# Two weight matrices cast to bf16 in flight by GpSimd's software DMA, in a linear-attention and MLP kernel on one core

## The chip, the cores and the metric

One NeuronCore of a Trainium2 chip. The time is that of the device for one execution, in microseconds (us), as the median of several executions. The profile's "span" is the stretch between the first and the last recorded instruction; it is 1.6 to 2.1 us shorter than the time. The record marks every run told here as fast: none is more than 1.5% above the quickest of its kernel.

## The reference, cut to what matters

```python
kv  = einsum('bhsd,bhse->bhde', k, v)            # batch 8, heads 8, s 576, d 64
out = einsum('bhsd,bhde->bhse', q, kv)
x   = out / rms(out) * g_norm                    # -> [8, 576, 512]
tok = einsum('ts,bsd->btd', w_tok, alpha1 * x + beta1)       # w_tok 576 x 576
u   = x + lam * tok
ch  = relu((alpha2 * u + beta2) @ w_ch1) @ w_ch2             # 512 x 2048, 2048 x 512
return u + lam * ch                              # float32
```

## The kernel before

All engines' work is put down as operations with their reads and writes, and a scheduler lays them out per engine. For the first batch (b=0) everything must be prepared: k, v and q loaded in halves, w_tok loaded and turned by matmuls with an identity, w_ch1 ("w1") and w_ch2 ("w2") loaded and cast. From the first matmul with w1 (called ch1 here) on, TensorE has real work without a break: ch1, the kv product of the second batch (b=1), the product with w2 (ch2), and so on.

```python
order = ["k0", "v0", "q0", "k1", "t0", "v1", "q1", "t1",      # SyncE's queue:
         "w0", "g", "w1", "w2", "Bk", "Bv", "t2", "w3", "Bq", "lam", "a2", "w4",
         "w5", "w6", "w7"]     # t: w_tok; w0-w3: w1's quarters; w4-w7: w2's; B: batch 1
...
def load_w(i):
    if i < 4:
        P.op("SP", 0.6, lambda e: e.dma_start(stg[:, i % 3], moe_w_ch1[...]), ...)
        for dj in range(4):                                   # casts on ACT, POOL or DVE
            P.op({"ACT": ..., "POOL": 0.66, "DVE": ...}, 0, lambda e, dj=dj: copy(
                e, w1[:, dj, 512 * i:512 * i + 512], stg[:, i % 3, dj]), ...)
        bias_groups(i)                                        # 16 matmuls, beta2 @ w1
    else:
        P.op("SP", 0.6, lambda e: e.dma_start(stg[:, i % 3], moe_w_ch2[...]), ...)
        for hh in range(4):                                   # w2 scaled by lam, on DVE or POOL
            P.op(dve_pool(512), 0, ...)
...
# kv product of one batch: 144 matmuls of 64x64, each with its weight load
m = e.matmul(t.ap(...), kf[rows, x, c], vf[rows, x, c], start=(c == 0), stop=(c == 8), ...)
...
# filler, put where TensorE would idle before ch1; a list of zeros
def warm(e, t):
    return e.matmul(t.flat()[:, 0:256], wz[:, 0:128], wz[:], start=True, stop=True)
```

## Time and profile before

| | before |
|---|---|
| time, median of 3 | 363.64 us (363.46 to 364.29) |
| span, granted clock | 362.2 us, 0.995 |
| first ch1 matmul | 33.89 us |
| kv product of b=1 starts | 43.13 us |
| first ch2 matmul | 58.31 us |
| end | 362.2 us |

The middle rows are milestones on TensorE. From 34 us on nothing on TensorE is filler, so a milestone that moves should move the end with it. The prediction below shows the busy totals, the stages and the chain.

```profile
q1 hardware_dynamic: 67472, 58.66, 59.7%
q8 instruction: 27, 0.44, 0.5%
```

### The profile page before, as it was taken

The page shows a single profiled execution, that of the slowest core. Times are in us where ns is not written, and L with a number is a line of the kernel's source. Part 1 is how long each engine was busy: PE and PEld are TensorE (multiplying, and loading weights), DVE is VectorE, ACT ScalarE, POOL GpSimd, SP SyncE. Part 2 cuts the span into 40 slices and gives each one's busy share as a digit, 9 for nine tenths or more (in the row PEclk, how much of TensorE's full clock was granted, in tenths as well). Part 3 has the DMA queues.
Part 4 walks back from the last instruction along what each step waited for, and adds up shares of the span by engine and source line. Part 5 has one row for each costly group of instructions (what it writes and reads, how often), then busy time and mean ns, then how long its engine had stood idle before and what let it go on. Part 6 is the DMA issues. An engine that isn't in the chain of part 4 may idle for free.

```text
span 362.2 us, 7967 instructions
## 1 busy us (share of the span) xinstructions
PE 353.6 (98%) x3543; PEld 213.6 (59%) x3335; DVE 207.1 (57%) x321; ACT 147.5 (41%) x262; POOL 113.1 (31%) x93
## 2 busy tenths in 40 slices
PE   7999999999999999999999999999999999999995
PEld 5888774467754554457744554457744554457644
DVE  3555799962876288723974289714883288620021
ACT  2576267037750168007830167007720156007500
POOL 4377078410252006700381016800751006300000
PEclk9899999999999999999999999999999999999999
DMA  7999996067947694667926692686746510341023
GB/s 282 364 375 338 376 365 223 0 73 128 315 156 119 107 313 162 88 128 117 381 47 134 111 352 88 116 119 194 288 66 128 115 29 2 72 93 24 2 58 87
DMA packets 67558, 59.17 MB, mean 163 GB/s; under 512 B 45552, under 2 KB 45828, under 8 KB 67524
## 3 DMA queue, kind: packets, MB, share of 16 engines
q1 hardware_dynamic: 67472, 58.66, 59.7%
q8 instruction: 27, 0.44, 0.5%
q14 instruction: 7, 0.06, 0.0%
q10 hardware_dynamic: 52, 0.01, 0.0%
HBM read 38.60 MB, written 9.44 MB: 133 GB/s over the span
## 4 chain that ended last, share of the span: by engine, by line
PE 93%; DMA 3%; DVE 1%; SPq 1%; issue 1%
PE ps L986 34%; PE ps L936 19%; PE ps L921 14%; PE ps L785 8%; PE ps L602 5%; DMA vf<-in_v_dram 3%; PE ps L397 2%; PE ps L682 2%; PE ps L1144 2%; PE ps L798 1%; PE ps L819 1%; PE ps L570 1%; PE ps L952 1%; DVE w L1268 1%; SPq L506 1%
## 5 line engine op out<-in xcount | busy, mean ns | idle before, releaser
L986 PE MATMUL ps<-w,ht 128*128 128x512 bf16 (+1 forms) x569 | 125.8, 373 | 1.8 <-issue 1.0
L986 PEld LDWEIGHTS ps<-w,ht 128*128 128x128 bf16 x592 | 56.8, 98 | 64.0 <-issue 1.2
L910 ACT ACTIVATE ht<-ps,bias 128x640 bf16<-128x640 f32 (+2 forms) x100 | 74.1, 744 | 45.8 <-PE ps L936 37.9
L936 PE MATMUL ps<-a2t,w 128*128 128x320 bf16 x512 | 71.5, 299 | 0.0
L760 POOL TENSOR_TENSOR xm<-xm,g_bc 128x1024 f32<-128x1024 f32 (+1 forms) x17 | 35.0, 2061 | 111.4 <-DVE rt L757 109.3
L936 PEld LDWEIGHTS ps<-a2t,w 128*128 128x128 bf16 x512 | 49.4, 98 | 20.2
L997 DVE TENSOR_TENSOR xm<-ps,xm 128x512 f32<-128x512 f32 (+1 forms) x33 | 22.2, 673 | 56.5 <-PE ps L986 56.4
L921 PE MATMUL ps<-a2t,w 128*128 128x512 bf16 x231 | 53.3, 380 | 0.9 <-DVE small L737 0.5
L633 ACT ACTIVATE kvd<-ps 64x256 bf16<-64x256 f32 x24 | 9.1, 378 | 101.2 <-PE ps L602 101.0
L731 DVE TENSOR_REDUCE small<-sq 128x16 f32<-128x1024 f32 (+3 forms) x30 | 25.1, 849 | 24.9 <-ACT sq L729 24.7
L921 PEld LDWEIGHTS ps<-a2t,w 128*128 128x128 bf16 x240 | 22.6, 98 | 25.7 <-DVE xm L753 0.7
L785 PE MATMUL ps<-rt,wt 128*128 128x512 bf16 x140 | 31.4, 379 | 0.0
L911 DVE TENSOR_SCALAR ht<-ps,bias 128x512 bf16<-128x512 f32 (+2 forms) x32 | 22.9, 725 | 11.4 <-PE ps L921 5.1
L729 ACT ACTIVATE sq<-ps 128x1024 f32<-128x1024 f32 (+3 forms) x30 | 21.6, 735 | 10.2 <-PE ps L397 8.2
L769 DVE TENSOR_TENSOR xm<-ps,xm 128x512 f32<-128x512 f32 x28 | 19.1, 686 | 8.0 <-PE ps L785 7.9
L785 PEld LDWEIGHTS ps<-rt,wt 128*128 128x128 bf16 x140 | 13.7, 98 | 16.5
L771 POOL TENSOR_TENSOR a2b<-xm,a_bc 128x512 bf16<-128x512 f32 x11 | 17.7, 1610 | 17.6 <-DVE xm L769 17.6
L534 POOL TENSOR_TENSOR qs<-qf,qs 128x512 bf16<-128x512 f32 x12 | 15.2, 1266 | 25.5 <-ACT qs L493 24.5
L997 DVE TENSOR_TENSOR xtl<-ps,xtl 128x512 f32<-128x512 f32 x4 | 2.8, 691 | 35.5 <-PE ps L986 35.5
L753 DVE TENSOR_TENSOR xm<-ps,small 128x1024 f32<-128x1024 f32 (+1 forms) x20 | 20.0, 1004 | 0.2
L602 PEld LDWEIGHTS ps<-vf,kf 64*64 64x64 f32 x1152 | 18.0, 137 | 3.5 <-issue 2.5
L602 PE MATMUL ps<-vf,kf 64*64 64x64 f32 x1152 | 19.3, 223 | 0.3 <-DMA vf<-in_v_dram 0.2
(105 smaller groups left out, 337.1 us busy)
## 6 DMA issues: line engine op xcount, KB each, us to landing
stg<-in_moe_w_ch_dram SPq DMA_DIRECT2D x8, 1024.0 KB, 10.9
kf<-in_k_dram SPq DMA_DIRECT2D x7, 1152.0 KB, 6.2
vf<-in_v_dram SPq DMA_DIRECT2D x7, 1152.0 KB, 9.2
qf<-in_q_dram SPq DMA_DIRECT2D x7, 1152.0 KB, 9.8
out_dram<-xm SPq DMA_DIRECT2D x62, 128.0 KB, 2.4
kf<-in_k_dram SPq DMA_DIRECT2D x2, 576.0 KB, 5.8
vf<-in_v_dram SPq DMA_DIRECT2D x2, 576.0 KB, 7.1
qf<-in_q_dram SPq DMA_DIRECT2D x2, 576.0 KB, 8.5
```

Source lines behind the costliest of these rows:

```text
L602: m = e.matmul(t.ap(slice(64 * i, 64 * i + 64))[:, y, 64 * x_:64 * x_ + 64], kf[rows, x, c], vf[rows, x, c], start=(c == 0), stop=(c == 8) ...
L729: P.op("ACT", act_us(64 * m), lambda e: e.activation(both(sqv), raw(), ACT.Square), r=[t], w=[("sq", sqs)])
L731: P.op("DVE", dve_us(64 * m), lambda e: e.tensor_reduce(out=smv, in_=sqv, axis=AX.X, op=ALU.add), r=[("sq", sqs)], w=[("sm", sms)], pri=-20)
L753: P.op("DVE", dve_us(64 * m), lambda e: e.tensor_tensor(out=x3, in0=raw(), in1=inv(), op=ALU.mult), r=[t, ("sm", sms)], w=xk, pri=-200)
L760: P.op(dve_pool(64 * m) if b < 2 else "POOL", pool_us(64 * m), lambda e: e.tensor_tensor(out=x3, in0=x3, in1=gb, op=ALU.mult), r=xk + ["g" ...
L785: m = e.matmul(t.flat(), wt[:, sc if sc < 4 else 4 + b % 2, 128 * c:128 * c + 128], rt[:, rs(b, sc), :], start=(sc == 0), stop=(sc == 4))
L910: return e.activation(dst, src(), ACT.Relu, bias=bi)
L911: return e.tensor_scalar(out=dst, in0=src(), scalar1=bi, scalar2=0.0, op0=ALU.add, op1=ALU.max)
L921: m = e.matmul(t.flat(), w1[:, dj, 128 * fj:128 * fj + 128], a2t[:, dj, 0:512], start=(dj == 0), stop=(dj == 3))
L936: m = e.matmul(t.ap()[:, i, 0:320], w1[:, dj, 128 * fj:128 * fj + 128], a2t[:, dj, 320 * i:320 * i + 320], start=(dj == 0), stop=(dj == 3))
L986: m = e.matmul(t.flat()[:, 0:m_], ht[:, fj, 128 * c:128 * c + 128], w2[:, fj, lo:hi], start=(fj == 0), stop=(fj == 15))
L997: P.op("DVE", dve_us(m_), lambda e: e.tensor_tensor(out=x, in0=t.flat()[:, 0:m_], in1=x, op=ALU.add), r=[t] + keys, w=keys)
```

## The change

Intent: w_tok and w1 leave SyncE's queue. GpSimd loads them with software DMAs that cast float32 to bf16 on the way, so the 16 casts of w1 vanish and w_tok can be turned by bf16 matmuls, one pass where float32 takes two. So that these loads get bandwidth, SyncE's loads of the second batch, and all that follow in its queue, are held until w1's second quarter is in.

```diff
@@ load of k, v, q
+                after=P.lastw[("w1", 1)] if b == 1 else [],
@@ SyncE's order
-        order = ["k0", "v0", "q0", "k1", "t0", "v1", "q1", "t1",
-                 "w0", "g", "w1", "w2", "Bk", "Bv", "t2", "w3", "Bq", "lam", "a2", "w4",
-                 "w5", "w6", "w7"]
+        order = ["k0", "v0", "q0", "k1", "v1", "q1",
+                 "g", "Bk", "Bv", "lam", "a2", "w4",
+                 "Bq", "w5", "w6", "w7"]
@@ w_tok (and its last part, wst4, likewise)
-                P.op("SP", 0.6, lambda e, u=u: e.dma_start(
+                P.op("POOL", 0.5, lambda e, u=u: e.dma_start(
                     wst[:, u, :], wrows[u % 2, :, u // 2:u // 2 + 7:2]),
@@ turning w_tok
-                                ident[0:rr, 0:rr], start=True, stop=True,
+                                identb[0:rr, 0:rr], start=True, stop=True,
@@ load_w, w1's quarters
-                P.op("SP", 0.6, lambda e: e.dma_start(stg[:, i % 3], moe_w_ch1[...
-                for dj in range(4):
-                    P.op({"ACT": ..., "POOL": 0.66, "DVE": ...}, 0, ... copy(...
+                P.op("POOL", 0.9, lambda e: e.dma_start(
+                    w1[:, :, 512 * i:512 * i + 512], moe_w_ch1[
+                        :, 512 * i:512 * i + 512].rearrange("(j p) f -> p j f", p=128)),
+                    w=[("w1", i)], dma_us=2.6, at=-9000.0 + i, after=P.lastw[gate[i]])
```

Cut: the bf16 tiles, the gates of the new loads, and the scheduler's model of a second DMA queue. Lines move by about 14: L602 is L616 after, L952 L966, L986 L1000, L1144 L1159, L1165 L1180, L1213 L1228, L1334 L1345.

## The prediction

> **What bounds the kernel now.** I read the page's first two parts first: one busy total per engine, then the forty slices.
>
> ```profile
> PE 353.6 (98%) x3543; PEld 213.6 (59%) x3335; DVE 207.1 (57%) x321; ACT 147.5 (41%) x262; POOL 113.1 (31%) x93
> PE   7999999999999999999999999999999999999995
> PEclk9899999999999999999999999999999999999999
> DMA  7999996067947694667926692686746510341023
> ```
>
> TensorE is busy throughout, so the end moves only if TensorE has less to do or starts its necessary work earlier. But some of "busy" is filler: the program multiplies zeros (L1334) to keep the clock up until the first ch1 matmul (L952). So next I read busy time by stage (the loads' first wait, the preparation up to ch1, the rest), and then the filler alone for the same stages:
>
> ```profile
> 0.00:13.50 13.50, 11.35 (x142) 9.14 (x142) 4.80 (x13) 5.33 (x12) 3.88 (x16) 1.00 0.88 320
> 13.50:34.00 20.50, 20.44 (x272) 17.99 (x273) 12.50 (x35) 13.72 (x32) 15.72 (x17) 0.92 0.98 347
> 34.00:362.00 328.00, 321.85 (x3133) 186.45 (x2921) 189.77 (x276) 128.43 (x218) 93.49 (x61) 1.00 0.57 146
> ```
>
> Columns: length, then busy time of PE, PEld, DVE, ACT, POOL, then granted clock, DMA share, GB/s. From 13.5 to 34 the DMA share is 0.98, TensorE is full at a mean clock of 0.92, and only 1.38 us of it is filler. After 34 us there is no filler, and about 6 us of 328 are idle, half of that after the last matmul. What can be won lies before 34 us, plus what leaves TensorE after it. The chain of waits shows how that stage is made up:
>
> ```profile
> 4.13 9.38 DMA vf<-in_v_dram
> 13.56 1.71 PE ps L602 x72
> 17.84 1.20 PE ps L1144 x16
> 20.09 3.14 PE ps L1144 x48
> 24.00 1.15 PE ps L1165 x8
> 34.03 3.51 PE ps L952 x32
> 41.37 1.12 PE ps L1144 x16
> 42.49 0.23 PE ps L1165 x2
> ```
>
> The second half of v arrives at 13.5, and from there to ch1 the chain is on TensorE without a break. L1144 and L1165 turn w_tok: 5.49 us before ch1 (1.20 + 3.14 + 1.15), 1.35 after it.
>
> Last, GpSimd in order of time, because the change puts eleven DMA issues on it:
>
> ```profile
> 14.77 1.27 POOL L757 TENSOR_TENSOR rt<-xm,e_bc 128x512 bf16<-128x512 f32 x1 [5.52 <-DVE xm L753]
> 20.60 2.66 POOL L760 TENSOR_TENSOR xm<-xm,g_bc 128x512 f32<-128x512 f32 x2 [1.76 <-DMA g_bc<-in_g_norm_dram]
> 28.06 0.72 POOL L757 TENSOR_TENSOR rt<-xtl,e_bc 64x256 bf16<-64x256 f32 x1
> 28.85 1.27 POOL L760 TENSOR_TENSOR xm<-xm,g_bc 128x512 f32<-128x512 f32 x1
> ```
>
> The last of these ends at 30.12. DVE adds the token product to its result from 31.1, so GpSimd has only 1 us of slack there.
>
> **What the Trainium skill says.** "DMA: Bandwidth & Descriptors", section "SWDGE vs HWDGE vs iDMA": a transfer that casts must be issued from GpSimd, whose cores write the descriptors in software. Its section "Issuing engines are not separate DMA queues": all issuers share the same 16 DMA engines and interleave. The trace before has no such transfer, so it shows neither; its 0.98 DMA share says there is no spare bandwidth for a second queue to find. "SBUF — State Buffer", section "SBUF: two separate sides", warns that descriptor writing starves while DVE runs a two-port copy; no run yet shows whether that happens here. "TensorEngine Tiling (Array Packing)", section "Restrictions": column tiling disables Fast Weight Load. These transposes use 64-column tiles, so I don't assume fast weights; the trace has L798's bf16 128x64 loads at a median of 110 ns.
>
> **The change, part by part.**
>
> *w_tok in bf16.* Forty transposing instructions leave 80 records at L1144: each f32 matmul runs as two passes, each with its weight load. In the 48-record stretch a pass takes 3.14/48 = 65 ns. In bf16 I expect one pass, of 65 ns if weight loading sets the pace and about 30 if the two column halves overlap fully; I take 50. With the five instructions of L1165, 45 x 0.05 = 2.2 us against 6.84: 4.6 us less, 3.7 before ch1 and 0.9 after.
>
> *Clock.* A window over 15 to 20 us shows a granted clock of 0.74, one over 10 to 15 shows 0.92: 5 x 0.26 + 5 x 0.08 = 1.7 us, in a stretch of f32 matmuls. With fewer of them I expect most of it back.
>
> *Moves on TensorE.* The order of instructions has the e_bc matmuls (L1044, 1.15 us, in the idle wait before 13.5 now) after the second kv product, and one more bias group (L1213, 0.38) ahead of ch1. TensorE alone would need 20.3 - 1.0 filler - 3.7 - 1.7 + 1.15 + 0.4 = 15.5 us from v's arrival to ch1, against 20.3.
>
> *Arrivals.* The six half-loads of k, v and q lead SyncE's queue, 0.59 MB each. At 368 to 395 GB/s that is 1.5 us each, and the f32 w_tok pieces no longer lie ahead of v. GpSimd's first w_tok load starts once q's first half is in (TensorE starts on it at 8.57), then shares the engines. I estimate v's second half at 12.5 to 13.5 (13.5 before), q's at 14 to 15.5 (15.6 before), w_tok complete near 16.5, w1's quarters from 19 on. Reads from HBM are unchanged in size; only the writes halve.
>
> *Casts of w1.* Sixteen 128x512 casts go: 9 on ScalarE at 620 ns (5.6 us) and 7 on GpSimd at 614 (4.3 us). None is on DVE, and those on GpSimd mostly follow the work ch1 waits for, so little of this reaches the end.
>
> *GpSimd's queue up to ch1.* It starts its rt product when e_bc is ready: at 15.4 to 16.4, later than 14.77, because e_bc moved. Then come two rt products (2.65), three issues (wst4, two quarters of w1; I allow 2.2), the tail (0.75), two g products (2.67), two rt products (2.65), the tail (0.78), two g products (2.67): 14.4 us, with its g-wait gone. It ends at 29.8 to 30.8, where it ends at 30.12 now. This cancels a large part of TensorE's gain. By then TensorE can have finished everything else, so from the last g product to ch1 remain DVE's adds, the transposes and the copies to a2t. I put the first ch1 matmul near 31.7, some 2.3 us earlier than 34.03.
>
> *After ch1.* 0.9 of transposes and 0.4 of the bias group are gone: 1.3. The b=1 loads are held until w1's second quarter is in, and q comes behind w2's first quarter; I subtract 0.2 for a wait there. The staging buffers now serve w2 alone; its quarters were not what TensorE waited for, so nothing is added.
>
> Sum: 2.3 + 1.3 - 0.2 = 3.4. I add 0.4 since DVE and ScalarE, relieved of casts and delays, should hand over the middle of the chain sooner: 3.8, so 359.8 us.
>
> **Rivals.**
>
> *A, TensorE's saving comes through whole.* If issues cost GpSimd well under 1 us, or the a2t chain overlaps better, ch1 starts near 28.5: 5.5 + 1.3 makes 357. For it: the unbroken PE chain. Against it: 1 us of slack on GpSimd.
>
> *B, GpSimd becomes the bound.* If a 512-row load holds GpSimd for 2 to 3 us, or it must wait for DMA progress before it can write more descriptors, the g products slip by that much and ch1 starts at 34 to 36: 362 to 365. For it: software descriptors, and 15.7 us of busy time in 20.5. Against it: 4.3 us of casts leave.
>
> *C, the loads merely change queue.* DMA is saturated up to 60 us either way. If the casting transfer runs at half rate, w1 arrives near 30, the held-back loads slip by 5 to 8 us and TensorE waits for b=1's k, v or q: 364 to 370. For it: nothing in this trace shows the casting rate. Against it: smaller writes.
>
> **Range and chances.** A and the main line fill 357 to 361; B takes it to 363. I give 356.9 to 362.8. Faster by over 2% needs 356.4, so 7.3 us, more than A's 6.8: 7%. Slower by over 2%, 370.9, needs C at its worst: 3%.
>
> **What would show it.** Turning w_tok in 40 plus 5 bf16 records of 30 to 65 ns spacing; no clock dip after 15 us; first ch1 matmul at 31 to 32.5; GpSimd without a gap from rt to the last g product, ending near 30; TensorE idle or filling more than 1.38 us just before ch1; some 4 us less TensorE work. I am wrong if ch1 starts before 29 (GpSimd was no limit), if it starts after 34 (issue cost), or if ch1 is early and the end is not (a load wait at b=1).

## More of the kernel before

```profile
43.13 2.33 PE L602 MATMUL ps<-vf,kf 64*64 64x64 f32 x144
```

Queue q8 carries instructions, not data: 27 transfers of 16 KB in the whole run, half a per cent of the DMA time. The second line is the kv product of b=1: 144 matmuls without a gap.

## The result, and the profile after

The time went up: 367.09 us (366.76 to 367.53, 4 runs) against 363.58 in the same rounds, a ratio of 1.0093 (95% interval 1.0075 to 1.0112). A ratio is the mean time of one kernel's fast runs over that of the other's of the same rounds, so not quite the ratio of the medians quoted.

| | before | after | predicted |
|---|---|---|---|
| first ch1 matmul | 33.89 | 33.27 | 31.7 |
| kv product of b=1 starts | 43.13 | 40.95 | |
| first ch2 matmul | 58.31 | 60.7 | |
| span | 362.2 | 365.4 | |

So the new kernel leads by 2.2 us when the kv product starts, and lags by 2.4 us when ch2 starts. The page after, the rows that stand for those shown of before:

```profile
PE 355.2 (97%) x3536; PEld 211.0 (58%) x3296; DVE 209.6 (57%) x319; ACT 142.6 (39%) x253; POOL 115.7 (32%) x97
PEclk9989989999999999999999999999999999999999
q1 hardware_dynamic: 64704, 53.14, 55.4%
q0 software_dynamic: 2768, 2.76, 4.8%
q8 instruction: 27, 0.44, 0.5%
```

The q0 row is new: the software DMAs. TensorE is busy for 1.6 us more than before, though it has less to do; matmuls that take longer at half clock would explain that, and the clock row has an 8 in the slices from 18.3 and from 45.7 us, where before had one from 9 us. The same by stage, with the columns as in the prediction; the third stretch, from ch1 to the end of a gap, is the new one:

```profile
13.50:33.27 19.77, 18.01 (x192) 15.19 (x192) 11.53 (x33) 10.10 (x26) 15.51 (x16) 0.91 1.08 231
33.27:46.50 13.23, 9.96 (x201) 7.55 (x199) 8.03 (x14) 2.52 (x6) 1.27 (x1) 0.99 1.04 379
```

TensorE is idle for 1.8 us of the first and 3.3 us of the second. The chain of waits says where:

```profile
12.36 9.74 DMA w<-in_moe_w_ch_dram
22.15 0.57 PE ps L1228 x16
...
41.29 1.94 PE ps L616 x122
43.23 3.27 issue
46.51 0.71 PE ps L616 x17
```

and TensorE's timeline, where brackets hold the idle time before the group and what ended it:

```profile
18.54 1.61 PE L1159 MATMUL ps<-identb,ht 128*64 128x128 bf16 x24
22.15 0.57 PE L1228 MATMUL ps<-b2hl,w 128*128 128x2 bf16 x16 [1.76 <-DMA w<-in_moe_w_ch_dram]
46.51 0.71 PE L616 MATMUL ps<-vf,kf 64*64 64x64 f32 x17 [3.27 <-issue]
```

Two waits, then. At 20.4 TensorE, in order, stands 1.76 us before the first bias group because w1's first quarter lands only at 22.1. And in the middle of the kv product, inside one loop of matmuls, it stops for 3.27 us with "issue" as the cause, which means that the profile shows nothing it waited for. The records put TensorE at half clock for 3.41 us from about the end of each, from 22.23 to 25.64 and from 46.12 to 49.53, which can cost up to 1.7 us each time. Before had one such window, 14.21 to 17.62. The Trainium skill, "TensorE: Matmul & The Clock Gate", section "Part 1: The HAM clock gate (the "warmup" mystery)", names a window of 3413 ns over which activity decides the clock; the lengths here agree. That the two waits brought the half clock is not shown: b_phase below has a stop of 2.94 us and no half clock behind it, while before (14.21), a_quiet (21.03 to 24.45) and a_over (20.92 to 24.34) have a half clock with no wait over 0.21 us in the 4 us ahead of it.

**What the stop is.** A loop whose inputs are all in does not wait for data halfway, so I looked at the one queue that carries no data, in the stretch of the stop:

```profile
q1 hardware_dynamic: 651, 1.29, 102.6%
q8 instruction: 1, 0.02, 2.0%
```

While the 16 engines are full of data (102.6%), one block of 16 KB of instructions comes in. I then counted TensorE's records in the trace (matmuls, weight loads and its few sequencer records) against the times of these transfers; the counts are mine, no view gives them. Before has 6,948 records and 27 transfers, one for every 257. So I set the first ten fetches of each trace against the moments when TensorE passes record 128, 384, 640, 896 and so on, every 256. Where the DMA engines were nearly empty, a fetch started 1.05 to 4.3 us after the crossing (16 cases, median 2.9); where they were full, mostly 4 to 8 us after it (68 of 90, median 5.3). And TensorE can run 320 records past the crossing; further it goes only once the fetch is in. In every stop of this case it went on 1.3 to 1.5 us after the fetch had landed. For the fourth fetch, counted from record 896, the limit is 1,216:

| | kv product: records | passes 896 at | fetch runs | reaches 1,216 at | stop |
|---|---|---|---|---|---|
| before | 1,041 to 1,329 | 36.72 | 41.82 to 42.87 | 44.42 | none |
| after | 958 to 1,250 | 38.28 | 44.09 to 45.19 | 43.02 | 3.27 us, at record 1,216 |

The kv product of b=1 passes 288 records in 2.3 us, far faster than anything else in this kernel. In before, record 1,216 falls inside it too, but the fetch has landed 1.55 us earlier, which by those 1.3 to 1.5 us is just enough. In after, each bf16 turning matmul is one matmul and one weight load where float32 was two of each, so 83 fewer records precede the product, in sum with small shifts of other groups; it begins sooner after the crossing, and it runs into the end of what has been fetched. The Trainium skill, "Perfetto Trace Analysis", section "Per-engine timelines", puts fetch and decode before the part of an instruction that the profiler reports; that agrees with a gap that no view explains.

### The profile page after: what moved, and what is told of

Same layout as the page of the kernel before. It is cut to its first block, busy times and chain, and to the rows that moved or that the text cites. A ratio compares the mean times of both kernels' runs of the same rounds, so it can differ in the third digit from the quotient of the medians.

```text
span 365.4 us, 7907 instructions
## 1 busy us (share of the span) xinstructions
PE 355.2 (97%) x3536; PEld 211.0 (58%) x3296; DVE 209.6 (57%) x319; ACT 142.6 (39%) x253; POOL 115.7 (32%) x97
## 4 chain that ended last, share of the span: by engine, by line
PE 86%; DVE 6%; DMA 4%; issue 2%; POOL 1%; ACTq 0%; ACT 0%; POOLq 0%; DVEq 0%
PE ps L1000 32%; PE ps L950 19%; PE ps L935 13%; PE ps L799 7%; PE ps L616 4%; DMA w<-in_moe_w_ch_dram 3%; PE ps L696 2%; PE ps L410 2%; PE ps L833 1%; DMA w<-in_moe_beta_dram 1%; DVE rt L771 1%; PE ps L812 1%; PE ps L966 1%; DVE small L745 1%; DVE w L1279 1%
## 5 line engine op out<-in xcount | busy, mean ns | idle before, releaser
L1000 PE MATMUL ps<-w,ht 128*128 128x512 bf16 (+1 forms) x592 | 128.9, 373 | 0.0
L1000 PEld LDWEIGHTS ps<-w,ht 128*128 128x128 bf16 x592 | 56.9, 98 | 63.9 <-issue 1.2
L774 POOL TENSOR_TENSOR xm<-xm,g_bc 128x1024 f32<-128x1024 f32 (+1 forms) x18 | 36.2, 2009 | 110.2 <-DVE rt L771 109.7
L950 PEld LDWEIGHTS ps<-a2t,w 128*128 128x128 bf16 x512 | 49.4, 98 | 20.4 <-DVE xm L767 0.3
L935 PE MATMUL ps<-a2t,w 128*128 128x512 bf16 x240 | 55.7, 383 | 0.0
L1011 DVE TENSOR_TENSOR xm<-ps,xm 128x512 f32<-128x512 f32 (+1 forms) x33 | 22.1, 672 | 52.3 <-PE ps L1000 52.3
L925 DVE TENSOR_SCALAR ht<-ps,bias 128x512 bf16<-128x512 f32 (+2 forms) x32 | 23.7, 746 | 11.8 <-PE ps L935 5.0
L548 POOL TENSOR_TENSOR qs<-qf,qs 128x512 bf16<-128x512 f32 x13 | 16.6, 1274 | 28.5 <-ACT qs L506 27.8
L616 PE MATMUL ps<-vf,kf 64*64 64x64 f32 x1152 | 19.5, 221 | 3.3 <-issue 3.3
L616 PEld LDWEIGHTS ps<-vf,kf 64*64 64x64 f32 x1152 | 18.1, 136 | 6.4 <-issue 6.2
```

Of the source, the lines that this page charges most:

```text
L616: m = e.matmul(t.ap(slice(64 * i, 64 * i + 64))[:, y, 64 * x_:64 * x_ + 64], kf[rows, x, c], vf[rows, x, c], start=(c == 0), stop=(c == 8) ...
L774: P.op(dve_pool(64 * m) if b < 2 else "POOL", pool_us(64 * m), lambda e: e.tensor_tensor(out=x3, in0=x3, in1=gb, op=ALU.mult), r=xk + ["g" ...
L925: return e.tensor_scalar(out=dst, in0=src(), scalar1=bi, scalar2=0.0, op0=ALU.add, op1=ALU.max)
L935: m = e.matmul(t.flat(), w1[:, dj, 128 * fj:128 * fj + 128], a2t[:, dj, 0:512], start=(dj == 0), stop=(dj == 3))
L950: m = e.matmul(t.ap()[:, i, 0:320], w1[:, dj, 128 * fj:128 * fj + 128], a2t[:, dj, 320 * i:320 * i + 320], start=(dj == 0), stop=(dj == 3))
L1000: m = e.matmul(t.flat()[:, 0:m_], ht[:, fj, 128 * c:128 * c + 128], w2[:, fj, lo:hi], start=(fj == 0), stop=(fj == 15))
```

## The experiments

Thirteen kernels in four batches, each batch on one chip with its own runs of the kernel before. All gave correct results.

### The stop: more instructions in front

Filler is the one thing whose instruction count can be changed without changing its work: a filler of 256 columns cut into four of 64 is 6 records more.

```diff
         def warm(e, t):
-            return e.matmul(t.flat()[:, 0:256], wz[:, 0:128], wz[:], start=True, stop=True)
+            warmed[0] += 1
+            n = 4 if warmed[0] <= 15 else 1          # a_phase: 15 (+90 records)
+            for i in range(n):
+                m = e.matmul(t.flat()[:, 256 // n * i:256 // n * (i + 1)], wz[:, 0:128],
+                             wz[:, 0:256 // n], start=True, stop=True)
+            return m
```

**a_phase**: the changed kernel with this.

> The changed kernel with only the first 15 zero fillers each cut into four of 64 columns: the same work, some 90 more TensorE instructions before the first load arrives. Theory (instruction fetch): the 3.3 us gap in the middle of the b=1 kv product is TensorE waiting for its next 16 KB of instructions, asked for at instruction 896 and delayed by the saturated DMA; 90 instructions earlier in the stream the request goes out some 6 us before, so the gap and the half-clock window after it go: 5.0 us faster than the changed kernel, about 362.1 (ratio to before 0.996). Rival (late data: the held-back k and v of b=1 come piece by piece): nothing changes, 367 and a gap at the same place.

Measured: 362.49 us (361.92 to 364.60), ratio 0.9989 (0.9965 to 1.0013). The kv product, records 1,048 to 1,340, has no gap; the fetch had landed at 38.33.

```profile
40.05 2.40 PE L616 MATMUL ps<-vf,kf 64*64 64x64 f32 x141
```

Its first bias group doesn't wait for w1 either, so not all of the 3.8 us against the changed kernel (ratio 1.0093 to 0.9989) need be the stop.

**b_phase**: the kernel before, with 21 fillers cut (126 records).

> The kernel before with the first 21 fillers cut into four: some 126 more instructions, the same work. Theory (instruction fetch): the request now falls just before the b=1 kv product (288 instructions in 2.3 us), so a gap of 1 to 4 us opens in or just after that product and the clock drops to half behind it: 365 to 369. Rival: no w_tok or w1 through GpSimd, so no gap, 363.6.

Measured: 367.85 us (366.30 to 369.56), ratio 1.0128 (1.0098 to 1.0159). The product lies at records 1,168 to 1,456 now, so it begins at the crossing of the fifth fetch (1,152) and is followed by a stop at record 1,472, which is 320 on:

```profile
42.58 2.33 PE L602 MATMUL ps<-vf,kf 64*64 64x64 f32 x144
44.84 0.42 PE L1187 MATMUL ps<-wt,smask 128*128 128x64 bf16 x5
45.19 0.55 PE L570 MATMUL ps<-ident,qf 128*128 128x128 f32 x3
48.68 0.55 PE L570 MATMUL ps<-ident,qf 128*128 128x128 f32 x3 [2.94 <-issue]
```

The same loss made in the kernel that never had it, by an edit that computes nothing. This profile also has ch1 at 32.8, ahead of before's 33.89, so the time lost is all behind it. The half clock that I expected behind the stop did not come in this execution. The six times follow the granted clock: 366.3 and 366.5 at 1.000, 367.7 and 368.0 at 0.995, 369.4 and 369.6 at 0.986.

**a_over**: 30 fillers cut, 180 records.

> The changed kernel with the first 30 fillers cut in four (180 more instructions for the same columns; the corrected version of the first batch had 90 more). Theory (instruction fetch): the burst of small matmuls of the second batch's kv product then begins near instruction 1,150, like the 1,168 of the kernel before with its 126 added, so TensorE stops again, 1.5 to 4 us, now just after the burst instead of inside it; ch1 starts as early as in the corrected version (32 to 33 us), and the time is 3 to 5 us above it: ratio to the kernel before 1.005 to 1.013. Rival (more instructions in the warm-up stretch help by themselves, or fillers in smaller pieces keep the clock): no stop, ratio 0.996 to 1.001 as with 90 added.

Measured: 362.90 us (362.02 to 364.66), ratio 0.9989 (0.9966 to 1.0012). I missed this: I expected a stop of 1.5 to 4 us, and it was 0.75 us.

```profile
46.14 0.60 PE L935 MATMUL ps<-a2t,w 128*128 128x512 bf16 x2 [0.75 <-issue]
```

It stands at record 1,470, where the rule puts it, but the product lay at 1,136 to 1,429, not at 1,150 as I had guessed: 41 slower records stood between its end and the limit, and they took so long that the fetch, 43.59 to 44.72, had landed before TensorE came to a stand at 45.39. It still stood until 46.14, 1.4 us after the landing. A few dozen records decide between a loss of 3 us and none.

**a_same** and **a_late**, on one chip: the changed kernel unaltered; and with fillers 33 to 47 cut (`32 < warmed[0] <= 47`) instead of the first fifteen, so that the first 12 us stay as they are.

> The changed kernel once more, unaltered, so that the next three can be compared with it on one chip in the same rounds. Every theory expects the stop of about 3.3 us in the second batch's kv product again (the fetch is a matter of instruction counts, and the queues are as full as before), the wait of 1 to 2 us for the first quarter of w1 at 20 us, and a ratio of 1.007 to 1.012. If the stop were an accident of one profile, the ratio would be under 1.003.

> The changed kernel with fillers 33 to 47 (the last fifteen before the main turning of w_tok, 12 to 20 us) cut in four instead of the first fifteen: the same 90 instructions, but the warm-up before 12 us is left as it was. Theory (the 90 instructions matter only through the place of the kv burst in the instruction stream): the kv burst begins near 1,055, no stop above 1 us there, ratio 0.996 to 1.004 whichever way the w1 wait falls; if the w1 wait of 1 to 2 us stays, ch1 starts near 33 us. Rival (the gain of the corrected version came from the start: fillers of the first 10 us in smaller pieces, an earlier arrival): the stop or an equal loss stays, ratio 1.006 to 1.012.

Measured: a_same 367.25 us (366.29 to 368.92), ratio 1.0112 (1.0089 to 1.0136), with a stop of 3.30 us at record 1,216 again; a_late 363.08 us (362.51 to 363.45), ratio 0.9988 (0.9976 to 1.0000), and this on TensorE:

```profile
21.71 0.55 PE L1228 MATMUL ps<-b2hl,w 128*128 128x2 bf16 x16 [0.27 <-DMA w<-in_moe_w_ch_dram]
40.71 2.40 PE L616 MATMUL ps<-vf,kf 64*64 64x64 f32 x141
```

No gap in the product, whose first three matmuls are listed apart. Its ch1 starts at 32.92, only 0.2 us before a_same's 33.12, so the gain lies behind that point. From ch1 to ch2 a_same takes 27.7 us and a_late 23.4: 4.2 us for the 3.3 us of stop and the half clock after it. The ratios differ by 0.0124, 4.5 us. But a_late's wait for w1 is 0.27 us where a_same's is 1.30, so these 4.5 us need not all hang on the place of the product; the pair a_bias and a_bias_late below changes that place alone.

### The stop: empty queues

**a_quiet**: nothing added to TensorE's stream, but SyncE's loads of w2 held until the kv product is done, and q of b=1 loaded ahead of them.

```diff
-                 "g", "Bk", "Bv", "lam", "a2", "w4",
-                 "Bq", "w5", "w6", "w7"]
+                 "g", "Bk", "Bv", "lam", "a2", "Bq", "w4",
+                 "w5", "w6", "w7"]
@@ load of w2's quarters
-                    at=sp["w%d" % i])
+                    at=sp["w%d" % i], after=P.lastw[("kvp", 0)] if n == 0 else [])
```

> The changed kernel with nothing added to its instruction stream (kv burst near instruction 958, where it stopped at 1,216 in two runs), but SyncE's four loads of w2 held until the second batch's kv product is done, and q of the second batch loaded ahead of them; so the DMA engines should run out of data near 37 us, before TensorE crosses instruction 896 at about 38 us. Theory (the stop needs both: the burst's place in the count and a fetch that comes late because the queues are full of data): the fetch starts within 2 us of the crossing, and the kv product has no stop above 0.5 us. What that saves is lost again to w2's later arrival, so the total time says little: ratio 0.998 to 1.012. Rival (the place in the instruction stream alone makes the stop, full queues or not): the stop of about 3.3 us at instruction 1,216 is there again, ratio above 1.008.

Measured: the stop shrank to 0.82 us, at the same record 1,216:

```profile
42.77 0.47 PE L616 MATMUL ps<-vf,kf 64*64 64x64 f32 x17 [0.82 <-issue]
```

TensorE passed record 896 at 37.20, sooner than I had reckoned, and the data drained until about 40.1; the fetch ran from 40.11 to 41.36, as soon as they were gone. It lagged 2.9 us instead of 5.8. My bounds (2 us, 0.5 us) are missed, but not the rival's 3.3 us: with the same count, less data in front makes a shorter stop. Both halves of the cause are needed for the whole stop. The time, 368.26 us (ratio 1.0114), is w2's price: VectorE scales w2 late, TensorE waits 3.15 us at 62.48 for VectorE's rt product, and the clock halves. It is no better kernel, as expected.

### The wait for w1

**a_bias**: the first bias group ordered behind the sums of w_tok; **a_bias_late**: that and the fillers of a_late.

```diff
-            P.op("PE", 0.6, f, r=[("w1", i), "b2", "b2h"], w=[t, ("bp", i)], pri=-30)
+            P.op("PE", 0.6, f, r=[("w1", i), "b2", "b2h"], w=[t, ("bp", i)], pri=-30,
+                 after=summed if i == 0 else [])
```

> The changed kernel with the first bias group of w1 ordered behind the sums of w_tok, and no added instructions (12 matmul instructions more from the fillers, 15 to 30 in the count). Theory: the wait for w1 at 20 us and the half clock after it are gone (1 to 3 us ahead of ch1, which starts 31.5 to 33 us), but the kv burst begins near 1,000, its end still lies beyond the 320 instructions after the request, so the stop stays, 1.5 to 3.5 us: ratio 1.002 to 1.009. Rival (the stop is caused by the w1 wait, through the delay or the clock, not by the instruction count): no stop, ratio 0.994 to 0.999 as with the 90 added.

> Both: the first bias group behind the sums and fillers 33 to 47 cut in four. Theory: no wait for w1 at 20 us, no stop in the kv product, ratio 0.993 to 1.000, like the earlier version with the first fifteen fillers cut (0.9968). Rival (where the cut fillers lie matters): above 1.002.

Measured, beside a_same and a_late: a_bias 365.83 us (364.59 to 367.69), ratio 1.0072 (1.0051 to 1.0094); a_bias_late 362.46 us (362.22 to 362.75), ratio 0.9976 (0.9963 to 0.9989). In a_bias the wait at 20 us is gone, and the stop is not:

```profile
40.89 1.85 PE L616 MATMUL ps<-vf,kf 64*64 64x64 f32 x111
45.84 1.22 PE L616 MATMUL ps<-vf,kf 64*64 64x64 f32 x33 [3.09 <-issue]
```

The product begins at record 994, 36 later than in after, and 111 instead of 124 of its matmuls in the long group come before record 1,216. So the stop isn't caused by the w1 wait or by the clock after it. The ratios put the w1 wait at 1.5 us (1.0112 to 1.0072), but the two intervals overlap, the six times of each kernel spread over 2.6 and 3.1 us, and the two profiled executions took the same (367.69 and 367.48), so no trace shows the gain: the wait's cost is not clear of noise. Between a_late and a_bias_late, where only 0.27 us of it was left, it is 0.4 us. The stop between a_bias and a_bias_late is clear: 0.0096, 3.5 us. a_bias_late has a small stop of its own that nobody planned: 0.82 us in the kv product of b=0, at record 449, which is 320 past the crossing of 128. **a_bias_ph** is the same pair in the first batch, with a_phase's fillers:

> The cut fillers as in a_phase, and the bias group of w1's first quarter must come after the sums of w_tok, so TensorE does not stand at 20.1 us for that quarter. Theory (the wait for w1 costs time on the path): 1.8 us of idle and 1.7 us of half clock go; 1.5 to 3 us faster than a_phase. Rival (GpSimd's g products, ending at 30.5, set the start of ch1 anyway): within 0.7 us of a_phase, the saved time turns into filler.

362.00 us (361.12 to 363.38), ratio 0.9968 (0.9945 to 0.9991), no gap in the kv product, ch1 at 32.8. That is 0.5 us under a_phase by the medians, 0.8 by the ratios: the 1.5 to 3 us that I expected are missed and the rival's 0.7 is about right. a_phase's profile has no wait for w1 that could go. These two are the only versions below the kernel before with an interval that excludes 1: by 0.2 to 0.3%.

### Holding the loads back

**a_nohold_ph**: a_phase with the hold taken out (`after=P.lastw[("w1", 1)] if b == 1 else []` removed).

> The cut fillers as in a_phase, and SyncE's k and v of b=1 no longer wait for w1's second quarter. If holding back costs (DMA idle between the queues, w2 late): 1 to 2 us faster than a_phase. If it protects w1: SyncE's queue is served first, as it was at 10 to 11.5 us, w1's quarters land some 5 us later, ch1 starts at 36 or later and it is 2 to 5 us slower than a_phase.

Measured: 367.33 us (366.81 to 368.04), ratio 1.0108 (1.0084 to 1.0133), 4.8 us over a_phase. w1 is later, TensorE waits, and half clock from 21.49 to 28.32 follows; ch1 starts at 36.73.

```profile
23.50 0.58 PE L1227 MATMUL ps<-b2hl,w 128*128 128x2 bf16 x16 [2.96 <-DMA w<-in_moe_w_ch_dram]
```

So holding SyncE back is not what made the change slow; without it the change is worse.

### One half of the change at a time

**x_wtok_ph8**: only w_tok by GpSimd in bf16, w1 as before, nothing held (8 fillers cut, so that the stop stays away). **x_w1**: only w1 by GpSimd with the hold, w_tok by SyncE and turned in float32.

```diff
 x_wtok_ph8, SyncE's order:
+        order = ["k0", "v0", "q0", "k1", "v1", "q1",
+                 "w0", "g", "w1", "w2", "Bk", "Bv", "w3", "Bq", "lam", "a2", "w4", ...]
 x_w1, SyncE's order:
+        order = ["k0", "v0", "q0", "k1", "t0", "v1", "q1", "t1", "t2",
+                 "g", "Bk", "Bv", "lam", "a2", "w4", "Bq", ...]
```

> Only w_tok by GpSimd in bf16 and turned by bf16 identity matmuls; w1 comes as in the kernel before (SyncE, float32, casts on the engines), nothing held back; the first 8 fillers cut in four, which puts the kv burst near the place it has in the kernel before. Theory (what is left of the change after the fetch stall is a preparation bound by the arrival of w1 and by the other engines, TensorE's saved time becoming filler): the cast DMA of w_tok now shares the queues with w1 in float32, w1 is no later than before, ch1 starts between 32.5 and 34.5 us, no stop above 1 us in the kv product, ratio 0.995 to 1.003. Rival (the bf16 turning is worth its 3.7 us ahead of ch1, as the prediction's sum has it, and w1's cast DMA takes it back): ch1 starts at 30 to 31.5 us, ratio 0.988 to 0.992.

> Only w1 by GpSimd in bf16, SyncE's later loads held back as in the change; w_tok comes by SyncE in float32 and is turned in float32. Its kv burst lies where that of the kernel before does, without adding instructions. Theory: the casts' removal and the late arrival of w1 nearly cancel, TensorE has 4.6 us more of turning to do, part of it after ch1: ch1 starts 33 to 35 us, no stop above 1 us in the kv product, ratio 0.997 to 1.006. Rival (the casts that left the engines are the gain that the corrected version keeps): ratio 0.993 to 0.997.

Measured: x_wtok_ph8 370.43 us (368.61 to 371.38), ratio 1.0186 (1.0161 to 1.0212), outside both expectations. x_w1 365.07 us (363.34 to 366.99), ratio 1.0048 (1.0017 to 1.0078), within mine: ch1 at 33.41, no stop above 0.15 us in the kv product of b=1 (one of 0.50 us in that of the third batch), full clock. In x_wtok_ph8 SyncE's float32 quarters of w1 compete with the cast loads; w_tok's pieces land late, and TensorE, in order, waits for them with its own work behind:

```profile
16.56 0.73 PE L1158 MATMUL ps<-identb,ht 128*64 128x128 bf16 x8 [1.81 <-DMA ht<-in_moe_w_tok_dram]
18.83 0.49 PE L1179 MATMUL ps<-identb,ht 128*64 128x128 bf16 x2 [1.54 <-DMA ht<-in_moe_w_tok_dram]
```

Its clock over 15 to 25 us is 0.64 and 0.68, and ch1 starts at 38.52. In before one queue's order put w_tok ahead of w1; with two queues nothing does. Neither half alone, as built here, gains anything. That w_tok's half needs the hold that came with w1 is likely from this and from a_nohold_ph, but no run tests w_tok's half with w1 held behind it.

### What is left for VectorE

**a_w4_ph**: a_bias_ph with w2's first quarter loaded before v of b=1, since VectorE, in order, waits for that quarter:

> The best version so far (first bias group behind the sums, 15 fillers cut) with SyncE's held loads in another order: the first quarter of w2 before v of the second batch instead of after it. Theory (the VectorE waits in order for the w2 quarter until 46 us, and TensorE for VectorE after it): the quarter lands 2 to 3 us earlier, ch2 starts 0.3 to 1.2 us earlier than in that version, ratio 0.990 to 0.996. Rival (VectorE is short of time in that stretch, not of data): ratio 0.996 to 0.999, unchanged.

Measured: 363.73 us (362.96 to 367.57), ratio 1.0029 (0.9992 to 1.0065): no gain, and the rival's 0.996 to 0.999 isn't met either. The quarter landed at 36.95, but its scaling then stood in front of ch1's output on VectorE, for which TensorE waited 1.24 us at 41.7, and ch2 started at 56.84 as in a_bias_ph (57.0). VectorE's work there is 4.8 to 5.0 us of every 5 between 50 and 65 us in before and in a_bias_late alike; it is short of time, not of data. These are the rows (VectorE is the third of the busy times) of that stretch, before first, then a_bias_late:

```profile
55.00:60.00 5.00, 4.93 (x23) 2.25 (x23) 4.81 (x11) 4.46 (x10) 4.68 (x5) 1.00 0.94 345
60.00:65.00 5.00, 5.00 (x24) 2.25 (x23) 4.83 (x9) 2.79 (x6) 4.23 (x3) 1.00 0.02 6
```

```profile
55.00:60.00 5.00, 5.00 (x24) 2.25 (x23) 4.94 (x9) 2.61 (x6) 4.68 (x5) 1.00 0.78 289
60.00:65.00 5.00, 4.79 (x22) 2.07 (x22) 4.81 (x8) 2.79 (x6) 4.64 (x4) 1.00 0.01 2
```

## Why the prediction was wrong, step by step

It said 359.8 us (356.9 to 362.8); it was 367.09, outside the range on the slow side.

**The step that failed** is "After ch1": 1.3 us gained, 0.2 lost, "so nothing is added". From ch1 to the end before takes 362.2 - 33.89 = 328.3 us, after 365.4 - 33.27 = 332.1: 3.8 us more, where 1.1 less was said. The runs put there an instruction fetch that comes too late for a burst, which none of the three rivals had: 3.5 us by a_bias and a_bias_late (1.0072 to 0.9976), 4.5 us at most by a_same and a_late.

Without the stop the step holds as far as ch2 only. From ch1 to ch2 it was 24.4 us before, 23.4 in a_late (32.92 to 56.35) and 22.9 in a_bias_late (32.77 to 55.7): 1.0 and 1.5 less, around the 1.1 said. But from ch2 to the end before takes 303.9 us, a_late 304.7 and a_bias_late 304.3: 0.4 to 0.8 given back, in the stretch where VectorE has no time left. That VectorE sets the pace there is argued from its busy time, not tested.

**w_tok in bf16** held. Forty records instead of 80; the 24 at 18.54 take 1.61 us by the view, 60 to 64 ns from one to the next, so 45 of them take about 2.9 us against 6.84. I had named 65 ns for a pace set by weight loads, 30 for full overlap, and took 50 and 2.2 us; it came out near the 65, whether or not weight loads are the reason, and 4.6 us less was 3.9. The pace per record stayed, the count halved, and this very halving moved the kv product in the instruction stream.

**Arrivals** was half wrong. "w1's quarters from 19 on" was 22.1 for the first and 24.4 for the second, and the order of instructions had the first bias group at 20. The prediction listed that group (0.4 us) and asked of it only its length. That is 1.76 us of waiting; a_bias puts it at 1.5 us of time, not clear of noise.

**Clock**: the window at 14 to 18 us went, as said, but two others came, at 22 and at 46 us. In a_late and a_bias_late the granted clock is 1.00 from 10 to 65 us; a_over and a_quiet have a half clock at 21 us without a wait. So fewer f32 matmuls were not enough to keep the clock up, and what brings it down the runs leave open.

**GpSimd's queue** held: its g products, which I put at 29.8 to 30.8, end at 30.5. The prediction's "eleven DMA issues" is a miscount: the change puts nine on it (five of w_tok, four of w1). Two DMA issues of w1 take 1.52 us together, wst4's 0.59.

```profile
12.36 1.52 POOL L1267 DMA_DIRECT2D w<-in_moe_w_ch_dram  x2
27.90 2.61 POOL L774 TENSOR_TENSOR xm<-xm,g_bc 128x512 f32<-128x512 f32 x2
```

**ch1 at 31.7** was 33.27, and 32.0 to 32.9 in the versions that have little of the wait (31.98 in a_quiet, whose profile happens to have none; a_phase 32.24, a_bias_late 32.77, a_late 32.92). I had allowed 1.4 us from the last g product to ch1, and a_bias_late takes 2.1. In a_late TensorE waits there for GpSimd's rt product (0.62 us) and for VectorE's add (0.60), so ch1 is bound by those two, as the main line said against rival A.

**Rival C's half rate** is false, its range of times was right for another reason. From 17 to 20 us the software queue writes 200 to 205 GB/s of bf16, so it reads about 400 GB/s of float32 (an estimate, twice what it writes), about as much as the 371 to 393 GB/s that the queues move in before from 20 to 30 us.

**Outside the span.** Time minus span, as the mean of each kernel's runs, is 1.61 to 1.63 us for before (40 runs in the four batches), 1.65 for b_phase, and 1.80 to 2.13 for every kernel with a software DMA. So the change costs some 0.2 to 0.5 us that no view of the profile holds; the prediction had no term for it. I did not find out what it is.

The terms together, as time: predicted -3.8; the stop and its clock +3.5 to 4.5; the w1 wait and its clock +1.5, not clear of noise; outside the span +0.4; 0.4 to 0.8 given back after ch2; ch1 bound 0.3 to 1.1 us later than said. That sums to +2.3 to +4.5, and measured is 0.0093 x 363.6 = +3.4. The terms overlap a little and none is exact to better than half a microsecond. What is shown: the stop needs the kv product's place in the instruction stream (seven kernels moved it, and the stop came and went with it), it ends 1.3 to 1.5 us after a fetch lands, and it gets shorter when the queues hold less data (a_quiet). What stays argued: that fetches wait in the DMA engines behind data asked for earlier. The counts of records are taken from the traces, where some records can be missing; the 128 and 320 are fitted to them, and so was the 256.

## What to carry to other kernels

Fewer instructions are not always less time: where a burst of tiny matmuls meets full DMA queues, look for a gap marked "issue" in the middle of a group, and shift the burst by some tens of instructions before trusting any comparison of two versions. When a change halves instruction counts early in a program, every later burst moves against the fetches, so a result of one per cent may say nothing about the change itself. A load that moves to another queue loses its place in the first queue's order; check what TensorE, in order, will stand before while it waits.

## What the Trainium skill lacked or had wrong

- "Runtime: NRT & Kernel Launch", section "Instruction fetch mechanics", has the fetch, and neither the prediction nor the rivals used it. It states blocks of 16 KiB, 256 instructions each, that the engine's sequencer fetches through a DMA queue of its own, and the runs agree (27 blocks for 6,948 records). But it calls the cost of crossing a block "mostly hidden" and gives TensorE room for 2,048 instructions. The runs show stops of 0.75 to 3.3 us at records 1,216 and 1,470 to 1,472, and one of 0.82 us at record 449, just past the crossing's 320 again; a room of 2,048 doesn't show in them. It lacks that a fetch starts later when the DMA engines are full of data: median 5.3 us after the crossing instead of 2.9.
- "DMA: Bandwidth & Descriptors", section "SWDGE vs HWDGE vs iDMA", says who must issue a casting transfer but not its rate: 200 to 205 GB/s of bf16 written here (17 to 20 us), with 0.56 to 0.64 us of GpSimd for an issue of 144 KB and 0.76 for one of 512 KB.
- The same page, section "Queues, rings and completion order", has each DMA engine take its queues in turn, a packet at a time. The turns in x_wtok_ph8 were not equal: over 12 to 15 us, with loads of both waiting, the trace has 405 packets of SyncE's queue (75% of the engines' time) and 163 of GpSimd's (33%). Whether the trace's packets are those of the page isn't known.
- No page that I found gives a cost of software DMA outside the profile's span: 0.2 to 0.5 us here (time minus span 1.80 to 2.13 us instead of 1.62).
